# Transposes by DMA, feed-forward in half batches at the lowest priority, and a mask shared by three engines, in a linear-attention and Fourier-mixing kernel

## The chip, the core and the metric

One core of a Trainium2 chip runs the whole program. The time is the device time of one execution in microseconds. For the kernel before it is 328.99 us, the median of three runs from 327.69 to 329.06.

## What is computed

The reference first runs a linear attention over four batches, eight heads, 768 time steps and a head dimension of 48. A state of 48x48 per head decays by w and takes in the outer product of k and v at each step:

```python
for t in range(S):
    cur = einsum('bhd,bhe->bhde', u * k[t], v[t])
    y[t] = einsum('bhd,bhde->bhe', r[t], state + cur)
    state = w * state + einsum('bhd,bhe->bhde', k[t], v[t])
```

The heads are then laid side by side, 384 columns, and go through a Fourier mixer and a feed-forward of width 1536:

```python
mixed = real(fft(fft(x, axis=1), axis=2))
u = x + mixed
un = (u - mean(u)) / sqrt(var(u) + 1e-6)
out = u + maximum(un @ w_ch1, 0) @ w_ch2
```

Inputs and output are float32.

## The kernel before

The kernel is written with a scheduler that takes the program as written, gives each instruction a priority by its place, and sets a fixed order of instructions for each engine ahead of time. Engines then run their own list in order and wait on semaphores. A tile pool with `bufs=n` gives n buffers, and who wants the next one waits until its last reader is done.

Attention goes in chunks of 128 time steps, six to a batch (`attention`, L163). A chunk loads k, r and v for all heads, 192 KB each, on SP's DMA queue (L175 to L177). DVE multiplies k by falling and r by rising powers of the decay (L180 KW, L181 RW), ACT casts v (L183), and POOL makes the diagonal term in three products (L185, L186, L190) with a sum by DVE between them (L188 DE). TensorE transposes KW and RW (L194, L196), and ACT copies the results out of PSUM (L198, L199, L201); for each pair of heads the transposed keys KB hold one head's rows and zeros for the other. TensorE makes the products of keys and queries (L208 A_ps), DVE multiplies both halves by a triangular mask (L211 MA), and TensorE adds up y from the state and the masked products (L217, L220). The next state is made in PSUM and scaled by DVE (L225, L229, L231 Sst). DVE adds the diagonal term (L233 X). From the fourth chunk on DVE also folds the finished chunk with the one three before it by sums and differences (L237 to L241, EO and XF), which halves the work of both Fourier steps.

The mixer (`mixer`, L245) makes the first Fourier step with 18 matmuls against tables (L254), ACT copies the results (L256 TT), and DVE makes a mirrored copy (L259 TR). Then for each of six blocks of 128 rows it runs the second step on TensorE (L273 to L277), and DVE adds the input (L279 UF), takes mean and variance (L282, L284), and norms (L287, L289 UN), with the root on ACT (L286); TensorE transposes the normed rows (L293) and ACT copies them (L294 UNT). The feed-forward of the whole batch follows: 72 matmuls into ReLUs on ACT (L300, L302 HT), 72 more (L306), and for each block a sum by DVE (L309 osb) and a store (L310).

What sets the order: the program emits attention of batch 0, the load of tables and weights, and then for each batch the attention of the next batch and the mixer of this one. The output tiles of the mixer's matmuls share three PSUM buffers (`mm`).

Of the kernel before, what the change touches and what calls it, by code (L numbers as in the profile page):

```python
# [9 lines left out]
AluOp = mybir.AluOpType  # L10
# [5 lines left out]
B = 4  # L16
H = 8
# [45 lines left out]
def kernel(  # L63
# [13 lines left out]
    inp = ctx.enter_context(tc.tile_pool(name="inp", bufs=7))  # L77
    ap_ = ctx.enter_context(tc.tile_pool(name="ap", bufs=3))
    bp = ctx.enter_context(tc.tile_pool(name="bp", bufs=2))
    psA = ctx.enter_context(tc.tile_pool(name="psA", bufs=1, space=bass.MemoryType.PSUM))  # L80
# [9 lines left out]
    wrow = cp.tile([128, H, D], F32, name="wrow")  # L90
    nc.sync.dma_start(out=wrow, in_=w.partition_broadcast(128))
    wT = cp.tile([128, NP], F32, name="wT")
    nc.vector.memset(wT, 1.0)
    wv = w.rearrange("(p a) d -> a d p", a=2)
    nc.scalar.dma_start(out=wT[0:D, :], in_=wv[0])
    nc.scalar.dma_start(out=wT[64:64 + D, :], in_=wv[1])
    urow = cp.tile([128, H, D], F32, name="urow")
    nc.scalar.dma_start(out=urow, in_=u.partition_broadcast(128))
    ident = cp.tile([128, 128], BF16, name="ident")
    nc.scalar.dma_start(out=ident, in_=id_c.ap())  # L100
    mtri = cp.tile([128, 128], BF16, name="mtri")
    nc.scalar.dma_start(out=mtri, in_=mtri_c.ap())
# [10 lines left out]
    lw = cp.tile([128, H, D], F32, name="lw")  # L113
    nc.scalar.activation(lw, wrow, Act.Ln)
    wpp = cp.tile([128, H, D], F32, name="wpp")
    wpn = cp.tile([128, H, D], F32, name="wpn")
    nc.scalar.activation(wpn, lw, Act.Exp, scale=ncol[:, 0:1])
    nc.scalar.activation(wpp, lw, Act.Exp, scale=icol[:, 0:1])  # L118
    lwT = cp.tile([128, NP], F32, name="lwT")
    nc.scalar.activation(lwT, wT, Act.Ln)  # L120
    wdec = cp.tile([128, NP], F32, name="wdec")
    nc.scalar.activation(wdec, lwT, Act.Exp, scale=float(L))
    WD = cp.tile([128, NP, 2, D], F32, name="WD")
    nc.gpsimd.memset(WD, 0.0)
# [3 lines left out]


    NB = 3  # L130
    RWs, KWs, KBs = [], [], []
    for i in range(NB):
        t = cp.tile([128, H, 64], BF16, name=f"RW{i}")
        nc.gpsimd.memset(t[:, :, D:64], 0.0)
        RWs.append(t)
        t = cp.tile([128, H, 64], BF16, name=f"KW{i}")
        nc.gpsimd.memset(t[:, :, D:64], 0.0)
        KWs.append(t)
    for i in range(2):
        t = cp.tile([128, NP, 2, 128], BF16, name=f"KB{i}")  # L140
        nc.gpsimd.memset(t, 0.0)
        KBs.append(t)
# [20 lines left out]
    def attention(b):  # L163
# [4 lines left out]
        for q in range(NQ):  # L168
# [9 lines left out]
            KW = KWs[i % NB]  # L178
            RW = RWs[i % NB]
            nc.vector.tensor_tensor(out=KW[:, :, 0:D], in0=kt, in1=wpn, op=AluOp.mult)  # L180
            nc.vector.tensor_tensor(out=RW[:, :, 0:D], in0=rt, in1=wpp, op=AluOp.mult)  # L181
            V = ap_.tile([128, H, D], BF16, name="V")
            nc.scalar.copy(V, vt)  # L183
            T1 = ap_.tile([128, H, D], F32, name="T1")
            nc.gpsimd.tensor_tensor(out=T1, in0=rt, in1=kt, op=AluOp.mult)  # L185
            nc.gpsimd.tensor_tensor(out=T1, in0=T1, in1=urow, op=AluOp.mult)  # L186
            DE = ap_.tile([128, H], F32, name="DE")
            nc.vector.reduce_sum(out=DE, in_=T1, axis=AX.X)  # L188
            TT = ap_.tile([128, H, D], BF16, name="TT")
            nc.gpsimd.tensor_tensor(out=TT, in0=V, in1=DE.unsqueeze(2).to_broadcast([128, H, D]), op=AluOp.mult)  # L190

            tp = psA.tile([128, 2, NP, 128], BF16, name="tp", bufs=1)
            for p in range(NP):
                nc.tensor.transpose(tp[:, 0, p, :], KW[:, 2 * p:2 * p + 2, :].rearrange("t h d -> t (h d)"), ident)  # L194
            for p in range(NP):
                nc.tensor.transpose(tp[:, 1, p, :], RW[:, 2 * p:2 * p + 2, :].rearrange("t h d -> t (h d)"), ident)  # L196
            KB = KBs[i % 2]
            nc.scalar.copy(KB[0:64, :, 0, :], tp[0:64, 0, :, :])  # L198
            nc.scalar.copy(KB[64:128, :, 1, :], tp[64:128, 0, :, :])  # L199
            RT = ap_.tile([128, NP, 128], BF16, name="RT")  # L200
# [147 lines left out]
```

## Time and profile before

| | |
|---|---|
| median of three runs | 328.99 us |
| profiled execution, its own time | 329.58 us |
| span of the profiled execution | 327.8 us |
| mean granted clock of TensorE | 0.77 |
| busy: TensorE, DVE, ACT, POOL | 220.3, 182.4, 134.9, 81.6 us |
| DMA moved | 23.14 MB, mostly in pieces under 512 B |

How to read it: the span runs from the first instruction to the last. A group of instructions shows its line, engine, operation, output and inputs, count, the busy time in us and the mean of one in ns, and then how long the engine stood idle just before them and what ended that. The chain of waits is followed back from the last instruction, at each step to what released it; its rows show start, length and the piece of work. A matmul's busy time overlaps that of its neighbours, so the time of a run of matmuls is read from the chain. A window's row shows its length, the busy time (and count) of TensorE, its weight loads, DVE, ACT and POOL, the granted clock, the DMA engines' share and GB/s.

### The profile page before, as it was taken

How to read it: one execution, taken by the hardware profiler on the slowest of the kernel's cores; microseconds unless marked ns; L12 is line 12 of the kernel's file. 1: busy time of each engine (PE TensorE's matmuls, PEld its weight loads, DVE VectorE, ACT ScalarE, POOL GpSimd, SP SyncE). 2: the span in 40 equal slices, each digit the busy share in tenths (PEclk: the TensorE clock that was granted, in tenths of full speed). 3: DMA queues.
4: the chain of work that ended last, by engine and by line, in shares of the span. 5: the costliest groups of instructions: out<-in, count | busy, mean ns of one | idle time of the engine just before them, and what ended most of it. 6: DMA issues, size and time to landing. Idle time of an engine off the chain costs nothing.

```text
span 327.8 us, 4361 instructions
## 1 busy us (share of the span) xinstructions
PE 220.3 (67%) x1616; PEld 145.2 (44%) x1616; DVE 182.4 (56%) x374; ACT 134.9 (41%) x272; POOL 81.6 (25%) x92
## 2 busy tenths in 40 slices
PE   0375467653666479996583799944459995446995
PEld 0365244442545256664462566622235652223662
DVE  0989598989989780249894502594430124442022
ACT  4552245633444239237452492331128504113910
POOL 5795365665437442012120200100000000000000
PEclk9999765965555559999757599995558998555999
DMA  7999999992447010120000001200000020000012
GB/s 151 218 187 186 269 206 194 221 184 50 98 86 155 1 24 2 48 98 0 2 1 0 2 0 50 97 0 0 2 0 0 25 97 24 0 0 3 0 48 96
DMA packets 81796, 23.14 MB, mean 71 GB/s; under 512 B 76144, under 2 KB 81008, under 8 KB 81776
## 3 DMA queue, kind: packets, MB, share of 16 engines
q1 hardware_dynamic: 78912, 20.26, 27.6%
q0 software_dynamic: 2016, 2.36, 4.4%
q10 hardware_dynamic: 848, 0.26, 0.3%
q8 instruction: 12, 0.20, 0.2%
q14 instruction: 8, 0.07, 0.1%
HBM read 20.52 MB, written 4.72 MB: 77 GB/s over the span
## 4 chain that ended last, share of the span: by engine, by line
PE 49%; DVE 28%; ACT 7%; DMA 7%; SPq 5%; issue 3%; ACTq 0%; DVEq 0%
PE mm L300 16%; PE mm L306 14%; DMA vt<-in_v_dram 4%; DVE MA L211 4%; PE mm L273 4%; DVE UF L279 3%; DVE UN L289 3%; DVE st L282 3%; PE mm L293 3%; DVE RW L181 3%; PE A_ps L208 2%; ACT RT L201 2%; SPq L175 2%; PE mm L277 2%; DVE KW L180 2%
## 5 line engine op out<-in xcount | busy, mean ns | idle before, releaser
L309 DVE TENSOR_TENSOR osb<-mm,UF 128x384 f32<-128x384 f32 x24 | 13.4, 558 | 87.7 <-PE mm L306 84.9
L300 PE MATMUL mm<-UNT,W 128*128 128x384 bf16 x288 | 54.3, 355 | 0.0
L302 ACT ACTIVATE HT<-mm 128x384 bf16<-128x384 f32 x96 | 46.8, 490 | 6.7 <-PE mm L300 6.5
L190 POOL TENSOR_TENSOR TT<-V,DE 128x384 bf16<-128x384 bf16 x24 | 20.6, 859 | 111.2 <-DVE X L233 48.2
L306 PE MATMUL mm<-W,HT 128*128 128x384 bf16 x288 | 47.5, 326 | 0.0
L293 PE MATMUL mm<-ident,UN 128*128 128x128 bf16 x72 | 12.0, 303 | 44.8 <-DVE UN L289 44.8
L300 PEld LDWEIGHTS <-W 128*128 128x128 bf16 x288 | 30.3, 106 | 21.8 <-issue 6.2
L306 PEld LDWEIGHTS <-HT 128*128 128x128 bf16 x288 | 28.2, 98 | 18.6
L208 PE MATMUL A_ps<-RT,KB 128*128 128x128 bf16 x192 | 21.3, 269 | 21.9 <-ACT RT L201 21.3
L211 DVE TENSOR_TENSOR MA<-A_ps,mtri 128x512 bf16<-128x512 f32 x48 | 31.4, 679 | 5.8 <-PE A_ps L208 5.8
L198 ACT COPY KB<-tp 64x512 bf16<-64x512 bf16 x24 | 13.9, 578 | 44.4 <-PE tp L196 42.4
L185 POOL TENSOR_TENSOR T<-rt,kt 128x384 f32<-128x384 f32 x24 | 27.5, 1144 | 16.8 <-DMA rt<-in_r_dram 12.9
L293 PEld LDWEIGHTS <-UN 128*128 128x128 bf16 x72 | 6.1, 126 | 51.6 <-DVE UN L289 51.1
L208 PEld LDWEIGHTS <-KB 128*128 128x128 bf16 x192 | 17.1, 121 | 25.4 <-issue 16.4
L279 DVE TENSOR_TENSOR UF<-mm,X 128x384 f32<-128x384 f32 x24 | 13.3, 554 | 26.5 <-PE mm L277 26.5
L186 POOL TENSOR_TENSOR T<-T,urow 128x384 f32<-128x384 f32 x24 | 26.9, 1124 | 1.5
L194 PE MATMUL tp<-ident,KW 128*128 128x128 bf16 x96 | 13.9, 294 | 18.6 <-DVE KW L180 16.0
L183 ACT CAST V<-vt 128x384 bf16<-128x384 f32 x24 | 12.2, 515 | 34.5 <-PE y_ps L220 22.6
L286 ACT ACTIVATE rstd<-mv,eps_t 128x1 f32<-128x1 f32 x24 | 7.1, 295 | 42.3 <-DVE mv L284 42.2
L294 ACT COPY UNT<-mm 128x384 bf16<-128x384 bf16 x24 | 11.5, 478 | 28.5 <-PE mm L293 28.5
L181 DVE TENSOR_TENSOR RW<-rt,wpp 128x384 bf16<-128x384 f32 x24 | 22.1, 920 | 0.5 <-ACT wpp L118 0.3
L180 DVE TENSOR_TENSOR KW<-kt,wpn 128x384 bf16<-128x384 f32 x24 | 21.8, 915 | 0.0
(65 smaller groups left out, 355.6 us busy)
## 6 DMA issues: line engine op xcount, KB each, us to landing
kt<-in_k_dram SPq DMA_DIRECT2D x24, 192.0 KB, 3.6
rt<-in_r_dram SPq DMA_DIRECT2D x24, 192.0 KB, 3.8
vt<-in_v_dram SPq DMA_DIRECT2D x24, 192.0 KB, 3.7
out_dram<-osb SPq DMA_DIRECT2D x24, 192.0 KB, 1.8
W<-in_moe_w_ch_dram POOLq DMA_DIRECT2D x6, 384.0 KB, 8.4
hid_t<-hid_c SPq DMA_DIRECT2D x1, 576.0 KB, 9.9
te_t<-te_c SPq DMA_DIRECT2D x1, 289.5 KB, 13.4
to_t<-to_c SPq DMA_DIRECT2D x1, 288.0 KB, 9.0
```

Of the source, the lines that this page charges most:

```text
L180: nc.vector.tensor_tensor(out=KW[:, :, 0:D], in0=kt, in1=wpn, op=AluOp.mult)
L181: nc.vector.tensor_tensor(out=RW[:, :, 0:D], in0=rt, in1=wpp, op=AluOp.mult)
L185: nc.gpsimd.tensor_tensor(out=T1, in0=rt, in1=kt, op=AluOp.mult)
L186: nc.gpsimd.tensor_tensor(out=T1, in0=T1, in1=urow, op=AluOp.mult)
L190: nc.gpsimd.tensor_tensor(out=TT, in0=V, in1=DE.unsqueeze(2).to_broadcast([128, H, D]), op=AluOp.mult)
L208: nc.tensor.matmul(A_ps[:, hh, :], lhsT=KB[:, p, hh % 2, :], rhs=RT[:, p, :], start=(hh == 0), stop=(hh == 3), skip_group_check=True)
L211: nc.vector.tensor_tensor(out=MA, in0=A_ps, in1=mtri.unsqueeze(1).to_broadcast([128, 4, 128]), op=AluOp.mult)
L279: nc.vector.tensor_tensor(out=UF[:, blk, :].rearrange("p (m a) -> p a m", a=2), in0=ps, in1=X[:, blk, :].rearrange("p (m a) -> p a m", a=2 ...
L293: nc.tensor.transpose(tps[:, dt, :], UN[:, dt * 128:(dt + 1) * 128], ident)
L300: nc.tensor.matmul(ps, lhsT=W1[:, dt, ft * 128:(ft + 1) * 128], rhs=UNT[:, dt, sh * 384:(sh + 1) * 384], start=(dt == 0), stop=(dt == 2))
L302: nc.scalar.activation(out=HT[:, ft, sh * 384:(sh + 1) * 384], in_=ps, func=Act.Relu)
L306: nc.tensor.matmul(ps, lhsT=HT[:, ft, sb * 128:(sb + 1) * 128], rhs=W2[:, ft, :], start=(ft == 0), stop=(ft == 11))
```

## The change

Eleven things change.

1. Keys and queries are written into one tile KR of twelve 128-column pieces, four for pairs of keys and eight for single queries with zeros in the other head's rows, and one DMA on SP's queue transposes it into KRT. The eight transposes of a chunk on TensorE and three copies on ACT go.
2. The R product is made in two halves (L176).
3. The products of keys and queries become four matmuls of 256 columns in place of eight of 128; the state's part of y becomes eight of 48 columns in place of four of 96.
4. The second half of the mask goes by an ACT copy (L204 AC) and a select on POOL (L205) instead of DVE.
5. From batch 1 on the fold runs once per batch, in four wide instructions.
6. The mixer's blocks go in halves of three: one root, one reciprocal and one scaled mean for three blocks (L282 to L285), the norm on ACT (L289), and one DMA transpose for the half (L291 UNT).
7. The feed-forward takes half a batch at a time (`mlp`).
8. Attention of later batches and the mixer (`fourier`) are emitted under a raised priority; attention of batch 0, the load of tables, and the feed-forward are not. The feed-forward of a batch is emitted one round later.
9. `mm` has four PSUM buffers instead of three; input tiles have five instead of seven.
10. The masks and u load on SP's queue after the first chunk, the decay's transposed rows on POOL's queue.
11. The decay's logarithm is taken in one ACT instruction of 388 columns.

The core of the diff:

```diff
-    inp = ctx.enter_context(tc.tile_pool(name="inp", bufs=7))
+    inp = ctx.enter_context(tc.tile_pool(name="inp", bufs=5))
...
+            K = KR[:, 0:4, :]
+            nc.vector.tensor_tensor(out=K.rearrange("t p (a d) -> t p a d", a=2)[:, :, :, 0:D],
+                                    in0=kt.rearrange("t (p a) d -> t p a d", a=2),
+                                    in1=wpn.rearrange("t (p a) d -> t p a d", a=2), op=AluOp.mult)
+            for a in range(2):
+                nc.vector.tensor_tensor(out=KR[:, 4 + a:12:2, a * 64:a * 64 + D], in0=rt[:, a::2, :],
+                                        in1=wpp[:, a::2, :], op=AluOp.mult)
...
+            nc.sync.dma_start_transpose(out=KRT, in_=KR.rearrange("t c d -> t (c d)"))
...
+                if g == 0:
+                    nc.vector.tensor_tensor(out=MA, in0=A_ps, in1=mtri.unsqueeze(1).to_broadcast([128, 4, 128]),
+                                            op=AluOp.mult)
+                else:
+                    AC = wp.tile([128, 4, 128], BF16, name="AC", bufs=2)
+                    nc.scalar.copy(AC, A_ps)
+                    nc.gpsimd.affine_select(out=MA, in_=AC, pattern=[[0, 4], [1, 128]], base=0,
+                                            channel_multiplier=-1, compare_op=AluOp.is_gt, fill=0.0)
...
+            for j in range(3):
+                nc.scalar.activation(out=UN[:, j, :], in_=UF[:, j, :], func=Act.Identity, scale=rstd[:, j:j + 1],
+                                     bias=nm[:, j:j + 1])
+            nc.sync.dma_start_transpose(out=UNT.rearrange("p j c t -> p (j c) t"),
+                                        in_=UN.rearrange("p j d -> p (j d)"))
...
-    st = attention(0)
-    load_tables()
-    for b in range(B):
-        nxt = attention(b + 1) if b + 1 < B else None
-        mixer(b, *st)
-        st = nxt
+    xs = [attention(0)]
+    load_tables()
+    hs = []
+    for b in range(B + 1):
+        with tc.high_priority(offset=5000):
+            if b + 1 < B:
+                xs.append(attention(b + 1))
+            if b < B:
+                hs.append(fourier(b, *xs[b]))
+        if b > 0:
+            for sh in range(2):
+                mlp(b - 1, sh, *hs[b - 1][sh])
```

What this moves, at the places of which the prediction speaks. On SP's queue before, the tables te, to and hid load right behind batch 0's chunks, and each chunk's kt, rt and vt follow:

```order
L175 DMA kt_462<-in_k_dram 128x8x48
L176 DMA rt_461<-in_r_dram 128x8x48
L177 DMA vt_463<-in_v_dram 128x8x48
L152 DMA te_t_120<-te_c 128x1158
L153 DMA to_t_121<-to_c 128x1152
L154 DMA hid_t_122<-hid_c 128x2304
L175 DMA kt_536<-in_k_dram 128x8x48
L176 DMA rt_535<-in_r_dram 128x8x48
```

Now SP's queue has, in the middle of batch 1, transposes of one chunk's KR between the loads of chunks six or seven further on:

```order
L181 DMA_TRANSPOSE KRT_588<-KR2_99 128x12x128
L165 DMA vt_1044<-in_v_dram 128x8x48
L163 DMA kt_1101<-in_k_dram 128x8x48
L164 DMA rt_1100<-in_r_dram 128x8x48
L165 DMA vt_1102<-in_v_dram 128x8x48
L181 DMA_TRANSPOSE KRT_646<-KR0_95 128x12x128
L163 DMA kt_1159<-in_k_dram 128x8x48
L164 DMA rt_1158<-in_r_dram 128x8x48
```

and the tables stand behind kt and rt of the very last chunk (kt_1900), with transposes of batches 2 and 3 behind them:

```order
L163 DMA kt_1900<-in_k_dram 128x8x48
L164 DMA rt_1899<-in_r_dram 128x8x48
L140 DMA te_t_104<-te_c 128x1158
L141 DMA to_t_105<-to_c 128x1152
L142 DMA hid_t_106<-hid_c 128x2304
L181 DMA_TRANSPOSE KRT_1169<-KR1_97 128x12x128
L165 DMA vt_1785<-in_v_dram 128x8x48
L181 DMA_TRANSPOSE KRT_1227<-KR2_99 128x12x128
L181 DMA_TRANSPOSE KRT_1629<-KR0_95 128x12x128
```

So the tables moved from ahead of batch 1 to behind all chunks' kt and rt. On DVE before, behind the last chunk's X, the blocks of a mixer go one by one from UF to UN:

```order
L233 TENSOR_TENSOR X_2100<-y_ps_2480,TT_2451 128x384
L259 COPY TR_2529<-TT2_2498 128x768
L237 TENSOR_TENSOR EO_2101<-X_2100 128x384
L238 TENSOR_TENSOR EO_2101<-X_2100 128x384
L279 TENSOR_TENSOR UF_2533<-mm_2535,X_1316 128x2x192
L239 TENSOR_TENSOR XF_2102<-EO_2101 128x2x192
L241 TENSOR_TENSOR XF_2102<-EO_2101 128x2x192
L282 BN_STATS st_2543<-UF_2533 128x6
L284 BN_AGGR mv_2545<-st_2543 128x2
L287 RECIPROCAL rstd_2547<-rstd_2547 128x1
L289 TENSOR_SCALAR UN_2550<-UF_2533,mv_2545,rstd_2547 128x384
```

Now on DVE, around the last chunk's X (y_ps_1931), stands the output sum osb of the feed-forward of batch 0; only osb_1471 of 24 comes ahead of it:

```order
L310 TENSOR_TENSOR osb_1471<-mm_1458,UF_840 128x384
L226 TENSOR_TENSOR X_1615<-y_ps_1873,TT_1859 128x384
L200 TENSOR_TENSOR MA_1922<-A_ps_1919,mtri_94 128x512
L226 TENSOR_TENSOR X_1615<-y_ps_1931,TT_1917 128x384
L310 TENSOR_TENSOR osb_1487<-mm_1474,UF_840 128x384
L236 TENSOR_TENSOR EO_1616<-X_1615 128x1152
L237 TENSOR_TENSOR EO_1616<-X_1615 128x1152
L239 TENSOR_TENSOR XF_1617<-EO_1616 128x6x192
L240 TENSOR_TENSOR XF_1617<-EO_1616 128x6x192
L310 TENSOR_TENSOR osb_1503<-mm_1490,UF_840 128x384
```

Twelve osb stood ahead of the last X before (batches 0 and 1); one does now. Where the tables are first needed, DVE has the fold of batch 1 (EO, XF) and then the TR copy of batch 0, with the product of chunk kt_1619 ahead of them:

```order
L186 TENSOR_REDUCE DE_1232<-T1_1229 128x8
L172 TENSOR_TENSOR KR0_95<-kt_1619,wpn_86 128x8x48
L236 TENSOR_TENSOR EO_468<-X_467 128x1152
L237 TENSOR_TENSOR EO_468<-X_467 128x1152
L239 TENSOR_TENSOR XF_469<-EO_468 128x6x192
L240 TENSOR_TENSOR XF_469<-EO_468 128x6x192
L256 COPY TR_836<-TT2_805 128x768 x3
```

That product frees the buffer for which the load of kt_1900, and so the tables behind it, waits.

234 lines of the change are left out of this document (108 added, 126 removed).

## Prediction

> **What bounds the kernel now.** I read the page first, then the busy time of the engines by stage, then the chain of waits in order of time, and last the groups of instructions. The page gives the sums:
>
> ```profile
> span 327.8 us, 4361 instructions
> PE 220.3 (67%) x1616; PEld 145.2 (44%) x1616; DVE 182.4 (56%) x374; ACT 134.9 (41%) x272; POOL 81.6 (25%) x92
> ```
>
> No engine is busy for the whole span, so the limit changes. The stages (length, then busy us of each engine, granted clock, DMA share, GB/s) say where:
>
> ```profile
> 0.00:36.00 36.00, 14.21 (x140) 12.46 (x140) 23.82 (x40) 14.02 (x25) 24.48 (x37) 1.00 1.06 198
> 36.00:76.00 40.00, 25.37 (x240) 17.72 (x240) 35.39 (x63) 18.44 (x36) 23.28 (x23) 0.68 0.96 194
> 76.00:120.00 44.00, 25.14 (x196) 19.11 (x197) 39.51 (x79) 17.08 (x34) 21.21 (x20) 0.50 0.38 75
> 145.00:185.00 40.00, 24.69 (x247) 18.73 (x244) 33.87 (x79) 19.56 (x41) 7.38 (x8) 0.73 0.02 6
> 270.00:298.00 28.00, 12.68 (x70) 7.28 (x69) 12.79 (x34) 7.19 (x17) 0.00 (x0) 0.60 0.02 7
> ```
>
> While attention runs (36 to 120, 145 to 185) DVE is the limit: 108.8 of 124 us, 88%. The first 76 us also keep the DMA engines full, at about 196 GB/s. From 270 to 298 nothing is even half busy. The chain of waits tells what that is, and what lies between the stages:
>
> ```profile
> 132.87 11.70 PE mm L306 x72
> ...
> 186.66 11.42 PE mm L300 x69
> ...
> 269.98 3.06 ACT TT L256 x6
> ...
> 273.71 0.57 DVE UF L279
> 274.30 0.57 DVE st L282
> ...
> 275.64 0.49 DVE UN L289
> ...
> 276.18 0.50 PE mm L293 x3
> ...
> 277.99 0.57 DVE UF L279
> ...
> 324.02 0.56 DVE osb L309
> ```
>
> Feed-forward: 72 matmuls of L306 take 11.70 us, 0.163 us each, and L300 the same (11.42 for 69). Four batches of 144 are 94 us in which PE alone works. The mixer: one block goes UF, statistics, UN, transpose, and the next UF starts 4.28 us later (273.71 to 277.99); six blocks run one after the other. Behind the last feed-forward matmul come 3.8 us (324.02 to the span's end).
>
> **The change part by part.** The order of the instructions divides the new program into two stages. Stage A ends with the last chunk's y matmul: on PE 57 of the 576 feed-forward matmuls stand ahead of it and 519 behind, and of the mixer batches 0 and 1 ahead, 2 and 3 behind. DVE does nearly everything else in A. So time = A + B, and the feed-forward fills little of A although PE has room there.
>
> *Stage A on DVE*, from these groups (busy us, mean ns):
>
> ```profile
> L211 DVE TENSOR_TENSOR MA<-A_ps,mtri 128x512 bf16<-128x512 f32 x48 | 31.4, 679 | 5.8 <-PE A_ps L208 5.8
> L181 DVE TENSOR_TENSOR RW<-rt,wpp 128x384 bf16<-128x384 f32 x24 | 22.1, 920 | 0.5 <-ACT wpp L118 0.3 <-DMA rt<-in_r_dram 0.2
> L180 DVE TENSOR_TENSOR KW<-kt,wpn 128x384 bf16<-128x384 f32 x24 | 21.8, 915 | 0.0
> L279 DVE TENSOR_TENSOR UF<-mm,X 128x384 f32<-128x384 f32 x24 | 13.3, 554 | 26.5 <-PE mm L277 26.5
> L282 DVE BATCH_NORM_STATS2 st<-UF 128x6 f32<-128x384 f32 x24 | 13.3, 556 | 0.5
> L233 DVE TENSOR_TENSOR X<-y_ps,TT 128x384 bf16<-128x384 f32 x24 | 13.1, 547 | 2.3 <-PE y_ps L220 2.1
> L188 DVE TENSOR_REDUCE DE<-T 128x8 f32<-128x384 f32 x24 | 12.9, 538 | 0.0
> L231 DVE TENSOR_TENSOR Sst<-u_ps,WD 128x384 bf16<-128x384 f32 x20 | 10.9, 544 | 1.8 <-PE y_ps L217 1.0 <-PE u_ps L229 0.7
> L238 DVE TENSOR_TENSOR EO<-X 128x384 bf16<-128x384 bf16 x12 | 5.6, 468 | 0.0
> L239 DVE TENSOR_TENSOR XF<-EO 128x384 bf16<-128x384 bf16 x12 | 5.3, 438 | 0.0
> L259 DVE COPY TR<-TT 128x768 bf16<-128x768 bf16 x12 | 4.9, 418 | 2.3 <-ACT TT L256 2.0
> L241 DVE TENSOR_TENSOR XF<-EO 128x384 bf16<-128x384 bf16 x12 | 4.8, 399 | 0.0
> L237 DVE TENSOR_TENSOR EO<-X 128x384 bf16<-128x384 bf16 x12 | 4.5, 375 | 0.0
> L284 DVE BATCH_NORM_AGGREGATE mv<-st 128x2 f32<-128x6 f32 x24 | 4.3, 177 | 0.5
> ```
>
> K product as before, 21.8. The R product becomes 48 halves: 0.46 each if it scales with its width, 0.92 if it doesn't at all, so 22 to 44. mv, nearly empty, takes 0.18, and with that as a fixed part a half takes 0.55; I take 0.50, hence 24. One mask of two stays: 15.7. DE, X and Sst stay: 36.9. Attention is 98.4. The fold is 20.2 (5.6 + 4.5 + 5.3 + 4.8); three of its four batches lie in A, 15.2, and wide instructions save a little: 14. Two of four batches of UF, st, mv and TR are half of 35.8, 17.9, with 1.4 for eight small ones at mv's 0.177. Sum: 132 us. The K and R rows hold a stall inside them:
>
> ```profile
> 44.25 1.10 DVE KW L180
> ...
> 61.20 0.47 DVE KW L180
> ```
>
> The same instruction takes 1.10 or 0.47, by my reading as POOL is busy or not. POOL does more than before, so I keep the means and count no gain.
>
> *Start.* The first product ran at
>
> ```profile
> 9.28 0.56 DVE L181 TENSOR_TENSOR RW<-rt,wpp 128x384 bf16<-128x384 f32 x1 [0.32 <-ACT wpp L118]
> ```
>
> Now ACT has the cast of V, which waits for vt, ahead of the logarithm of the weights; everything queued on ACT waits with it. I put this at 1.2 us, a guess that enters the sum as it is: 10.5.
>
> *Waits.* At the 88% of the windows above, 132 us of DVE take 150. One stall comes on top: the tables load behind the last chunks' loads, whose buffers wait for DVE, and soon after DVE stops at the TR copy, which needs 18 matmuls and six ACT copies made from those tables. A landing between the 1.8 and 8.4 of the DMA rows further on, 5; 18 matmuls at half clock, twice 0.163, 5.9; the last copy, 0.5; less 4.9 of folding meanwhile: 7 us. A = 10.5 + 150 + 7 = 168.
>
> *Mask by ACT and POOL.* Each chunk adds an ACT cast of 512 columns (0.51 per 384 in the chain: 0.68) and a POOL select, which the trace doesn't show:
>
> ```profile
> L190 POOL TENSOR_TENSOR TT<-V,DE 128x384 bf16<-128x384 bf16 x24 | 20.6, 859 | 111.2 <-DVE X L233 48.2 <-DVE mv L284 27.1 <-DVE rstd L287 19.2
> L185 POOL TENSOR_TENSOR T<-rt,kt 128x384 f32<-128x384 f32 x24 | 27.5, 1144 | 16.8 <-DMA rt<-in_r_dram 12.9 <-DVE DE L188 3.8
> L186 POOL TENSOR_TENSOR T<-T,urow 128x384 f32<-128x384 f32 x24 | 26.9, 1124 | 1.5
> L141 POOL MEMSET KB<- 128x1024 bf16 x2 | 1.8, 948 | 0.0
> ```
>
> Per 512 columns: 0.47 by the memset, 1.53 by L185. I take 1.0, as one operand lies between none and two. POOL then has 75.0 + 24 = 99 us of A's 168: hidden. At 1.5 it has 111 and is hidden too. ACT loses three copies of a chunk and gains the cast; nothing waits for it.
>
> *Transposes by DMA.* Each chunk sends 128x1536 bf16, 384 KB, through SP's queue between the loads. No transpose is in the trace. The nearest rows:
>
> ```profile
> kt<-in_k_dram SPq DMA_DIRECT2D x24, 192.0 KB, 3.6
> out_dram<-osb SPq DMA_DIRECT2D x24, 192.0 KB, 1.8
> W<-in_moe_w_ch_dram POOLq DMA_DIRECT2D x6, 384.0 KB, 8.4
> ```
>
> Loads move 198 GB/s with the engines full, so 192 KB hold them 0.99 us and a chunk's three loads 2.97. At that rate a transpose holds them 1.98 us (lower end). The W row has the same 384 KB and lands after 8.4 (upper end, though its wait in line is in it). I take 2.0, nearest to the loads of the same queue: 24 x (2.97 + 2.0) = 119 us, under the 157 that A leaves after its start. The cover ends where 24 x (2.97 + t) exceeds 157: t = 3.6. Behind a waiting transpose stand the next chunks' loads and, at the end of A, the tables. Removed on PE are eight transposes per chunk and three per block; PE was not the limit there, so nothing counts.
>
> The Trainium skill, "VectorE: DVE Perf Modes", section "The three transpose paths", puts a 128x128 transpose at 1309 ns by DMA against 390 on TensorE and advises TensorE where the output may go to PSUM. Twelve blocks one after the other would be an estimated 15.7 us, and the sum 10.5 + 24 x 18.67 + 113.6 = 572. The skill's "Advanced Engine Details and Errata", "X-Bar Transpose (TRN2)", says the opposite, as fast as a regular DMA, which is my 2.0; no run here shows either yet.
>
> *Stage B.* 519 matmuls x 0.163 = 84.6. Mixers 2 and 3 stand between them: the first step as in the chain (269.45 to 273.71 there; 4.2 us, held by six ACT copies of 0.51), then six blocks without the 4.28 us loop, since the norm and the transpose come later and feed-forward matmuls run meanwhile. A block's 768 columns twice are 0.65 us at L306's rate, 3.9 for six, at most six UFs slower: 5. Together 2 x 9.2 = 18.4. The UN products (6 x 0.49 per batch) now run on ACT among the ReLUs that pace L300: 5. End 3.8. B = 111.8. If that cover failed and the loop came back, it would cost 2 x 6 x 4.28 = 51 less the 10 counted.
>
> *Sum.* 168 + 111.8 = 279.8 against the profiled span of 327.8. The profiled execution took 329.58, 1.8 more than its span, and 0.2% more than the median of 328.99. 279.8 + 1.8 = 281.6: I say 282.
>
> **The rivals.** *The DMA queue paces A.* For: it was full for 76 us with loads alone. Against: before, the loads ran ahead of need; here they spread over A. With t = 5, A = 10.5 + 24 x 7.97 = 202 and the time 202 + 111.8 + 1.8 = 316.
>
> *Slower: the transpose holds the queue beyond 5.6 us.* One mechanism: SP's queue takes transposes and loads in order, and a slow transpose keeps loads, hence DVE, hence all else waiting. It decides where A exceeds 329.6 - 113.6 = 216, so 205.5 / 24 - 2.97 = 5.6 us. At 8.4, A is 283 and the time 397. Against: 8.4 includes queueing behind full engines. "VectorE: DVE Perf Modes" of the Trainium skill, "The three transpose paths", lies on this side.
>
> *Better than counted.* If DVE has no gaps and the tables come early, A = 143; with mixers at column rate B = 102; time 246. Against: DVE never passed 90% here.
>
> *It doesn't do what it says.* The feed-forward has the lowest priority but 519 of its matmuls run after attention, as serially as before; that is already in the sum. If also the mixer chain stayed exposed (41 us), the time would be 323; the order speaks against that.
>
> **How the numbers follow.** Forecast 0.62 (DVE paces A). DMA paces A, t between 3.6 and 5.5: 0.18. Transpose above 5.7: 0.11. Better than 256: 0.06. No change (t near 5.6, or the chain exposed): 0.03. Range: 256 is DVE busy at 95% with no table stall and no ReLU term (10.5 + 139 + 106.8); 316 is t = 5. It holds the first two cases, 0.80. Faster 0.62 + 0.18 + 0.06 = 0.86, within 0.5% 0.03, slower 0.11; half a per cent is about what a measurement of this kernel tells from no change.
>
> **What would show it.** A ends near 168 us with DVE about 88% busy until then; a transpose takes near 2 us of the queue, and DVE's idle time at MA is small; PE is full from there with two breaks of about 9 us; TR in the first mixer waits about 7 us. I am wrong if SP's or the DMA queue's share of the chain in A is large, if the transpose row shows over 3.6 us, or if UN or UNT ends PE's waits in B.

## The result, and the profile after

The changed kernel takes 293.87 us (median of four, 292.54 to 296.78) against 329.02 us for the kernel before in the same comparison: ratio 0.895, 95% interval 0.887 to 0.903. The profiled execution took 292.54 us for a span of 290.8. Forecast were 282 us and a range of 256 to 316. Medians in this document take in every execution, also the slow one of e5 below, which took 334.80 us where the other three took 286.12 to 287.07.

The profiled spans differ by 37 us, and one place shows where they came from: the last X of attention, at which stage A ends, before and then after (times of the first and the last start):

```profile
L233 DVE TENSOR_TENSOR X<-y_ps,TT x24: 536/546/558, 18.0 to 217.6; 128x384 bf16<-128x384 f32 x24
```

```profile
L226 DVE TENSOR_TENSOR X<-y_ps,TT x24: 527/554/559, 23.0 to 181.6; 128x384 bf16<-128x384 f32 x24
```

Stage A ends 36 us earlier. What follows (B) has the same length, 110.2 us before (327.8 - 217.6) and 109.2 after.

This does not mean that attention became faster. Before, 288 feed-forward matmuls started ahead of the last X, now 59 do. At 0.163 us each the 229 that moved are 37 us, which is all by which A is shorter (an estimate, which takes them as run alone). The gain is that B takes them in at the same length: its feed-forward is 84 us instead of 47, so all else in it, with two mixers in both kernels, is 25 us instead of 63. Which part of the change did that (the halves, the norm on ACT, the order) was not taken apart.

The page of after, first its sums, then busy tenths in 40 slices, then the share of the two large DMA queues:

```profile
span 290.8 us, 3776 instructions
PE 178.5 (61%) x1336; PEld 110.2 (38%) x1336; DVE 152.2 (52%) x318; ACT 105.5 (36%) x208; POOL 97.5 (34%) x113
PE   0034123011643264098654697999699996999995
DVE  0494459816977589339799885519210290201202
DMA  6899999999988999910962409310501104201102
q1 hardware_dynamic: 126448, 32.32, 53.8%
q0 software_dynamic: 2080, 2.36, 5.4%
```

PE is nearly full from slice 24 on. In the first 17 slices it is mostly under half busy, DMA is full, and DVE is not. By stage (length, then busy us of PE, PEld, DVE, ACT, POOL, granted clock, DMA share, GB/s), the last row being A from its first product to its end:

```profile
12.00:36.00 24.00, 8.00 (x71) 5.02 (x71) 15.77 (x28) 2.93 (x6) 13.80 (x17) 1.00 1.10 179
36.00:76.00 40.00, 10.17 (x87) 6.93 (x87) 25.59 (x46) 5.28 (x10) 25.03 (x27) 1.00 1.04 198
76.00:120.00 44.00, 16.65 (x157) 11.35 (x158) 33.67 (x61) 8.16 (x15) 25.87 (x28) 1.00 0.97 188
11.25:182.10 170.85, 77.86 (x714) 50.07 (x715) 121.06 (x238) 45.90 (x90) 89.27 (x100) 0.95 0.84 158
```

No engine is busy for more than 71% of A: DVE works 121.06 of 170.85 us and stands idle for 49.8. Before, it was busy for 88% of the stretches in which attention ran. Most of the idle time lies early: 31.3 us of it ahead of the twelfth X, which starts at 110.7 us. In the kernel before, the twelfth X started at 81.5 us, with 8.2 us idle since 11.25. What DVE waited for in A (total, times, longest), and three waits that lie behind it:

```profile
DVE DE L186 <- POOL TT L188: 10.2, 5, 5.2
DVE TR L256 <- ACT TT L253: 9.0, 1, 9.0
DVE X L226 <- PE y_ps L214: 8.2, 9, 1.9
DVE MA L200 <- PE A_ps L195: 6.3, 4, 2.4
DVE KR L172 <- DMA KRT<-KR: 4.6, 3, 3.0
...
PEld L195 <- DMA KRT<-KR: 33.8, 16, 7.0
PE mm L251 <- DMA te_t<-te_c: 9.3, 1, 9.3
ACT V L179 <- DMA vt<-in_v_dram: 26.0, 6, 15.4
```

One wait is that of the tables (TR, 9.0 us, from te_t). The others are smaller, and behind them stand two things: a chunk's transpose, for which PE's weight loads waited 33.8 us, and late loads: the longest wait of DE, 5.2 us, ends with a V whose cast had waited 15.4 us for vt. Two stretches show it best:

```profile
54.00:69.50 15.50, 1.32 (x10) 0.66 (x10) 6.36 (x11) 1.53 (x3) 13.61 (x15) 1.00 1.03 204
118.00:123.50 5.50, 0.01 (x1) 0.00 (x1) 0.60 (x1) 0.00 (x0) 0.00 (x0) 1.00 1.06 250
```

In the second all engines stop until the tables land. In the first, POOL alone is busy most of the time. SP's rows there show why: eight loads of vt are issued from 57.66 us on, and three transposes only behind them. DVE stood from 57.6 to 62.89 for the first of these vt, PE until 69.47 for the first KRT.

```profile
57.66 7.30 SPq L165 DMA_DIRECT2D vt<-in_v_dram  x8
...
65.01 5.88 SPq L181 DMA_TRANSPOSE KRT<-KR  x3
```

The transposes themselves (median us from issue to landing), beside the chain's end (start, us):

```profile
KRT<-KR SPq DMA_TRANSPOSE x24, 4.1
UNT<-UN SPq DMA_TRANSPOSE x8, 3.2
```

```profile
243.31 3.08 PE mm L301 x18
246.40 5.85 PE mm L307 x36
252.25 5.85 PE mm L301 x36
...
281.50 5.86 PE mm L307 x36
287.36 0.02 issue
287.38 0.56 DVE osb L310
```

Stage B runs at the forecast's rate: 36 matmuls in 5.85 us, 0.163 each, without a break between these runs. PE's only wait in it (182 us to the end) is

```profile
PE mm L301 <- ACT HT L303: 4.6, 4, 1.4
```

### The profile page after: what moved, and what is told of

Its sections match the earlier page's. It is cut to its first block, busy times and chain, and to the rows that moved or that the text cites. A ratio compares the mean times of both kernels' runs of the same rounds, so it can differ in the third digit from the quotient of the medians.

```text
span 290.8 us, 3776 instructions
## 1 busy us (share of the span) xinstructions
PE 178.5 (61%) x1336; PEld 110.2 (38%) x1336; DVE 152.2 (52%) x318; ACT 105.5 (36%) x208; POOL 97.5 (34%) x113
## 3 DMA queue, kind: packets, MB, share of 16 engines
q1 hardware_dynamic: 126448, 32.32, 53.8%
## 5 line engine op out<-in xcount | busy, mean ns | idle before, releaser
L310 DVE TENSOR_TENSOR osb<-mm,UF 128x384 f32<-128x384 f32 x24 | 13.3, 555 | 68.6 <-PE mm L307 68.4
L195 PE MATMUL A_ps<-KRT 128*128 128x256 bf16 x96 | 22.7, 381 | 30.9 <-DMA KRT<-KR 28.6
L204 ACT CAST AC<-A_ps 128x512 bf16<-128x512 f32 x24 | 14.0, 585 | 60.4 <-PE A_ps L195 60.4
L176 DVE TENSOR_TENSOR KR<-rt,wpp 128x192 bf16<-128x192 f32 x48 | 26.0, 573 | 3.5 <-DMA rt<-in_r_dram 3.2
L172 DVE TENSOR_TENSOR KR<-kt,wpn 128x384 bf16<-128x384 f32 x24 | 18.7, 784 | 15.6 <-ACT wpn L111 9.8
L205 POOL TENSOR_SCALAR_AFFINE_SELECT MA<-AC 128x512 bf16<-128x512 bf16 x24 | 16.8, 702 | 26.0 <-ACT AC L204 21.1
L195 PEld LDWEIGHTS <-KRT 128*128 128x128 bf16 x96 | 10.4, 125 | 38.3 <-DMA KRT<-KR 33.8
L214 PE MATMUL y_ps<-V,MA 128*128 128x48 bf16 x192 | 12.4, 205 | 15.6 <-DVE MA L200 9.2
L253 ACT CAST TT<-mm 128x386 bf16<-128x386 f32 (+1 forms) x24 | 12.4, 594 | 22.5 <-PE mm L251 22.5
L200 DVE TENSOR_TENSOR MA<-A_ps,mtri 128x512 bf16<-128x512 f32 x24 | 16.4, 682 | 7.6 <-PE A_ps L195 6.3
L186 DVE TENSOR_REDUCE DE<-T 128x8 f32<-128x384 f32 x24 | 13.1, 545 | 12.0 <-POOL TT L188 10.2
```

The lines of the kernel that those rows point to most:

```text
L172: nc.vector.tensor_tensor(out=K.rearrange("t p (a d) -> t p a d", a=2)[:, :, :, 0:D], in0=kt.rearrange("t (p a) d -> t p a d", a=2), in1=w ...
L176: nc.vector.tensor_tensor(out=KR[:, 4 + a:12:2, a * 64:a * 64 + D], in0=rt[:, a::2, :], in1=wpp[:, a::2, :], op=AluOp.mult)
L195: nc.tensor.matmul(A_ps[:, 2 * pp:2 * pp + 2, :], lhsT=KRT[:, p, :], rhs=KRT[:, 4 + 2 * p:6 + 2 * p, :], start=(pp == 0), stop=(pp == 1), ...
L200: nc.vector.tensor_tensor(out=MA, in0=A_ps, in1=mtri.unsqueeze(1).to_broadcast([128, 4, 128]), op=AluOp.mult)
L205: nc.gpsimd.affine_select(out=MA, in_=AC, pattern=[[0, 4], [1, 128]], base=0, channel_multiplier=-1, compare_op=AluOp.is_gt, fill=0.0)
```

## The experiments

Twelve kernels were run, each an edit of the changed kernel. A comparison has its own runs of the kernel before; so kernels are compared by their ratios to it. The table has them all, with the start of the last X, what the span has behind it (B), and DVE's busy and idle time from 11.25 us to that X's end:

| kernel | median us | ratio, 95% interval | last X | B | DVE busy / idle in A |
|---|---|---|---|---|---|
| before | 329.02 | 1 | 217.6 | 110.2 | 147.4 / 59.4 |
| changed | 293.87 | 0.895 (0.887 to 0.903) | 181.6 | 109.2 | 121.1 / 49.8 |
| e1 thin v | 290.13 | 0.881 (0.877 to 0.884) | 180.1 | 107.7 | 122.2 / 47.2 |
| e2 two transposes | 316.77 | 0.962 (0.952 to 0.971) | 203.3 | 108.7 | 122.4 / 70.2 |
| e6 weights late | 303.65 | 0.923 (0.918 to 0.927) | 191.6 | 110.5 | 121.0 / 59.9 |
| e8 transposes by ACT | 313.52 | 0.952 (0.948 to 0.956) | 200.9 | 109.9 | 121.7 / 68.4 |
| e9 look-ahead 2 | 293.33 | 0.893 (0.888 to 0.898) | 185.2 | 104.9 | 127.9 / 46.7 |
| e10 look-ahead 3 | 297.96 | 0.905 (0.899 to 0.912) | 186.1 | 111.4 | 132.1 / 43.3 |
| e3 tables in the middle | 282.52 | 0.860 (0.856 to 0.864) | 176.3 | 106.6 | 121.8 / 43.9 |
| e5 transposes by TensorE | 286.69 | 0.872 (0.868 to 0.877) | 169.7 | 114.7 | 125.5 / 33.6 |
| e4 mask on DVE | 304.92 | 0.928 (0.921 to 0.934) | 196.1 | 105.5 | 134.3 / 51.2 |
| e11 half of R | 291.90 | 0.887 (0.881 to 0.894) | 181.6 | 109.5 | 108.3 / 62.5 |
| e7 no priority | 274.12 | 0.833 | 189.4 | 81.7 | 136.3 / 42.5 |
| e12 tables and TensorE | 281.30 | 0.855 (0.850 to 0.860) | 164.6 | 114.9 | 126.9 / 27.1 |

e1's first product ran only at 14.33 us, so 3.1 us of its idle time are its later start. For e7 no interval was given; its four executions, 269.86 to 276.94 us, all lie below every execution of the others (280.23 the lowest).

**First question: do bytes, DVE or SP's order pace A?** e1 takes bytes away and leaves the issues:

```
-            nc.sync.dma_start(out=vt, in_=v[b, :, sl, :].rearrange("h p d -> p h d"))
+            nc.sync.dma_start(out=vt[:, 0, :], in_=v[b, 0, sl, :])
-            nc.scalar.copy(V, vt)
+            nc.scalar.copy(V, vt[:, 0:1, :].to_broadcast([128, H, D]))
```

> Of v only the first head is loaded (24 KB instead of 192 KB a chunk) and ACT spreads it over the eight heads of V, so the output leaves out seven of the eight heads of v; every DMA is still issued, and SP's order is nearly the same. Removed are 24 x 168 KB, at 196 GB/s 20.6 us of the 16 DMA engines. Three theories of what paces stage A of the changed kernel (293.9 us; A ended at 182 us in its profile). The bytes (loads, transposes and weights keep the engines full until about 123 us): A ends about 20 us earlier, 274 us (270 to 279). DVE, as predicted, with the transfers hidden: 291 to 294 us. The order on SP's queue (instructions that wait there for KR or for a buffer, with the next issues behind them): the order and the waits stay, so no more than 5 us, 289 to 294.

Measured 290.13 us: 1.6% less than the changed kernel by the ratios, not 7%. The edit also moved two casts of V ahead of the logarithm on ACT, which is why its first product ran 3.1 us later; from its first product on, A gained 4.6 us. That is still far from 20: the bytes alone do not pace A. e1's row for 36 to 76 us is

```profile
36.00:76.00 40.00, 10.33 (x93) 6.95 (x94) 28.23 (x47) 5.19 (x10) 23.68 (x26) 1.00 0.93 176
```

with 176 GB/s where the changed kernel had 198, and DVE at 28.23 us instead of 25.59.

e2 adds bytes and issues:

```
+            KR2 = wp.tile([128, 11, 128], BF16, name="KR2", bufs=1)
+            nc.sync.dma_start_transpose(out=KR2, in_=KR[:, 0:11, :].rearrange("t c d -> t (c d)"))
```

> Every KR is transposed a second time by DMA (11 of its 12 pieces, 352 KB) into a tile that nobody reads; the result stays as it is. At 2.2 us of all engines for 384 KB (66 us more of the queue for 32 transposes than before the change) that is 24 x 0.917 x 2.2 = 48 us of transfers, and 24 x 1.8 = 43 us in which SP issues. The bytes pace A: 340 us (328 to 346). DVE paces A: by the prediction's cover (24 x (2.97 + t) against 157, so t = 3.6) the doubled t of 4.0 goes 10 us over it, so 300 to 308. SP's order paces A: 320 to 340. It separates DVE from the other two, not these from each other.

Measured 316.77 us, 23 more (20 by the faster two of its four executions), between the cases: more than the 14 at most for DVE alone, less than the 34 to 52 for the bytes. A became 21.7 us longer, DVE's busy time stayed (122.4) and its idle time rose by 20.4. So a further transpose is not hidden, although neither bound holds in full. Two side effects blur the price: te now stood earlier on SP's queue (issued at 88.90 us), and KR2 has one buffer, for which SP waited 8.7 us in six waits.

e6 moves the weights:

```
+    def load_weights(X):
+        for dt in range(3):
+            nc.gpsimd.tensor_copy(W1[0:1, dt, 0:1], X[0:1, 5, 0:1])
+            nc.gpsimd.tensor_copy(W2[0:1, 4 * dt, 0:1], X[0:1, 5, 0:1])
```

> W1 and W2 (15.7 us of the engines on POOL's queue) are loaded only after the last X of batch 1, instead of during batch 0: six copies of one element on POOL make the loads wait. The result stays as it is. SP's queue is untouched. The bytes pace A: 15.7 us of transfers leave the time in which the engines are full, 279 us (276 to 284), unless feed-forward matmuls then wait for weights in A, which costs nothing as few stand there. DVE paces A: 291 to 294. SP's order paces A: 291 to 294.

Measured 303.65 us, 10 slower, which no theory gave. The weights now came at 107 to 113 us, right ahead of the tables, and the wait for these grew from 9.3 to 21.9 us, seen in e6's row:

```profile
PE mm L256 <- DMA te_t<-te_c: 21.9, 1, 21.9
```

So the whole time of this run doesn't price the bytes: they still stood ahead of the tables, in a worse place. Up to there it does say something. Without the weights among the first loads the fifth X started at 39.8 us instead of 47.2, and the twelfth at 104.4 instead of 110.7: 6 to 7 us, which came with 15.7 us of transfers moved. By e1 and e6 together, bytes pace a part of A, and not most of it.

e8 puts the transposes on another queue:

```
-            nc.sync.dma_start_transpose(out=KRT, in_=KR.rearrange("t c d -> t (c d)"))
+            nc.scalar.dma_start_transpose(out=KRT, in_=KR.rearrange("t c d -> t (c d)"))
```

> The 24 transposes of KR are issued by ACT instead of SP (1.8 us each in the changed kernel, so up to 43 us of ACT, which is busy for 54 of A's 182 us); loads are no longer queued behind a transpose that waits for KR, nor transposes behind loads that wait for a buffer. The result and the bytes stay as they are. The bytes pace A: 290 to 296. DVE paces A: 290 to 296. SP's order paces A: the waits on SP for KR, A_ps and y_ps in A (about 60 us in all, part of them overlapping other idle time) go, 273 to 284.

Measured 313.52 us, 20 slower. It does not tell whether SP's order costs anything, for it put new waits in the place of the old. SP's rows in A of e8:

```profile
SPq L291 <- DMA KRT<-KR: 38.4, 3, 18.9
SPq L165 <- ACT V L179: 29.5, 7, 17.9
SPq L163 <- DMA KRT<-KR: 15.6, 3, 8.4
```

SP waited for transposes of the other queue to land before it issued its own (L291), and a transpose landed after 5.7 us (median) instead of 4.1. Inconclusive for its question.

**Second question: SP's bunches, the tables, or the transpose itself?** e9 and e10 keep the loads of chunk i behind the transpose of chunk i - 2 or i - 3:

```
+            with tc.issue_after(trs[i - 2]) if i >= 2 else nullcontext():
                 nc.sync.dma_start(out=kt, in_=k[b, :, sl, :].rearrange("h p d -> p h d"))
...
-            nc.sync.dma_start_transpose(out=KRT, in_=KR.rearrange("t c d -> t (c d)"))
+            ti = nc.sync.dma_start_transpose(out=KRT, in_=KR.rearrange("t c d -> t (c d)"))
```

> The loads of chunk i are issued only behind the transpose of chunk i - 2 on SP (a constraint on the order of issue; no wait for the transpose to land). The bytes and the result stay as they are; the order of SP becomes at most two chunks of loads between transposes instead of up to eight, and the tables are issued right behind chunk 1's loads. Three runs have weakened the theory that the bytes pace A (21 us of transfers less gave 4 us, not 20), and doubled transposes cost 23 us where DVE alone would have cost 10. Theory now: the order on SP; in the changed kernel eight loads each of k, r and v stand ahead of three transposes, and between 53 and 69 us DVE stands still because those transposes are issued only from 65.0 on. By that theory A ends 12 to 20 us earlier, 270 to 282 us, the tables' 9 us in it. If the bytes pace A: the tables move 6 us of transfers to the front and only the gap of 9 us goes: 284 to 294. If DVE paces A: 284 to 288, the table stall alone. If a shorter look-ahead starves DVE of loads: over 296.

> As the run before, with the transpose of chunk i - 3: at most three chunks of loads between transposes, and the tables late, behind chunk 17's loads, as in the changed kernel. The result stays as it is. SP's order paces A: between the changed kernel and the look-ahead of two, 278 to 288 us. The bytes or DVE pace A: 290 to 296, since neither bytes nor tables move.

Measured 293.33 and 297.96 us: neither differs from the changed kernel by more than the intervals allow, and e9 had its tables at 8.30 us. The theory of the bunches, which expected 270 to 288, fell in these two. DVE's busy time in A also grew, by 6.8 and 11.0 us; most of that is the R products, 34.4 and 36.0 us in sum instead of 27.5. With few loads ahead SP waits for the products instead, with the next loads behind it, and DVE for A_ps; of e9:

```profile
SPq L183 <- DVE KR L178: 60.3, 22, 6.8
```

```profile
DVE MA L203 <- PE A_ps L198: 24.0, 13, 4.3
```

e3 moves the tables alone, by a dependence on the third X of batch 0:

```
+    def load_seq(X):
+        for t in (te_t, to_t, hid_t):
+            nc.gpsimd.tensor_copy(t[0:1, 0, 0:1], X[0:1, 2, 0:1])
```

> The three loads of the tables (1.15 MB, 6 us at 196 GB/s) are issued after the third X of batch 0, among the loads of chunk 6 instead of behind chunk 23's; three copies of one element on POOL set the moment. The result stays as it is. It measures the prediction's table stall (7 us) by itself: PE waited 9.3 us for te in the changed kernel and DVE 9.0 at TR. If the stall is what it costs: 284 to 288 us. If the bytes pace A the 6 us only move, and loads come 6 us later: 288 to 294. SP's order: the bunch of 24 loads ahead of three transposes stays, so no more than the stall: 284 to 288.

Measured 282.52 us, 11 less than the changed kernel; the profiled spans differ by 7.9. That is the stall and a little more. te is issued at 37.70 us instead of 118.98, DVE's idle time in A falls by 5.9, A by 5.3 and B by 2.6, of which 1.1 are 7 more feed-forward matmuls ahead.

e5 gives KR's transposes back to TensorE:

```
+            for g in range(2):
+                tp = ps.tile([128, 6, 128], BF16, name="tp", bufs=1)
+                for c in range(6):
+                    nc.tensor.transpose(tp[:, c, :], KR[:, 6 * g + c, :], ident)
+                nc.scalar.copy(KRT[:, 6 * g:6 * g + 6, :], tp)
```

> KR is transposed by TensorE, six pieces into one tile of PSUM, copied by ACT to KRT, twice a chunk; the transposes of UN stay with the DMA, and mm has three buffers instead of four. The result stays as it is. PE gets 288 transposes more (about 0.1 to 0.16 us each, 29 to 46 us), ACT 48 copies of 768 columns (about 0.9 us, 43 us), both engines less than half busy in A. 53 us of transfers go, and SP issues loads alone. The bytes pace A: 262 to 275. SP's order paces A: 268 to 282, since no transpose waits behind loads. DVE paces A: 288 to 296. If the copies on ACT come into the chain of each chunk: over 296.

Measured 286.69 us: 7 less than the changed kernel, but 5 above what SP's order would give and 1 below DVE's case. Added were (busy us, mean ns)

```profile
L184 PE MATMUL tp<-ident,KR 128*128 128x128 bf16 x288 | 36.4, 277 | 27.8 <-DVE KR L172 13.8 <-ACT KRT L185 7.9 <-DVE KR L176 5.7
L185 ACT COPY KRT<-tp 128x768 bf16<-128x768 bf16 x48 | 38.4, 800 | 39.0 <-PE tp L184 38.4 <-PE y_ps L215 0.4
```

and still A became 11.9 us shorter: DVE was idle for 33.6 us instead of 49.8, and busy for 4.4 us more. ACT's casts of V waited 5.0 us for vt instead of 26.0, so the loads came earlier too. B became 5.5 longer: only 22 feed-forward matmuls stand ahead of the last y, 35 fewer, and 35 x 0.163 = 5.7.

**Third question: is it DVE after all?** e4 gives DVE 24 products more, e11 24 fewer:

```
-                if g == 0:
...
-                    nc.gpsimd.affine_select(out=MA, in_=AC, pattern=[[0, 4], [1, 128]], base=0,
-                                            channel_multiplier=-1, compare_op=AluOp.is_gt, fill=0.0)
+                nc.vector.tensor_tensor(out=MA, in0=A_ps, in1=mtri.unsqueeze(1).to_broadcast([128, 4, 128]),
+                                        op=AluOp.mult)
```

> The whole mask goes back to DVE: 24 products more of 512 columns at 0.68 us, 16.4 us of DVE, and 24 casts on ACT and 24 selects on POOL fewer. The result, the bytes and the order on SP stay as they are. If DVE paces A, as predicted: 16 to 23 us more (16.4 us at a DVE that is busy 72 to 100% of A), 310 to 317 us. If A is paced by no engine's work but by waits between the engines in their fixed orders: 290 to 300, as DVE has some 50 us of waiting in A to put the products into, and the step over ACT and POOL goes.

```
-            for a in range(2):
+            for a in range(1):
                 nc.vector.tensor_tensor(out=KR[:, 4 + a:12:2, a * 64:a * 64 + D], in0=rt[:, a::2, :],
```

> The second of the two R products of a chunk is left out, so the odd heads of R are zero in the result: 24 DVE instructions of 0.57 us, 13.8 us, fewer; the rest, the bytes and nearly all of SP's order stay. If DVE paces A: 14 to 19 us less, 275 to 280 us. If waits between the engines pace A: 288 to 295.

The rows of A, e4 first:

```profile
11.25:196.70 185.45, 83.38 (x728) 52.51 (x729) 134.30 (x263) 33.26 (x66) 72.36 (x77) 0.82 0.79 145
```

```profile
11.25:182.10 170.85, 79.75 (x713) 50.32 (x714) 108.30 (x213) 46.78 (x91) 89.35 (x101) 0.96 0.85 157
```

e11 is the plainest reading of the study: DVE works 12.8 us less, its idle time grows by 12.7, and the last X starts at 181.6 us as before the edit (291.90 us, 2 less, within the intervals). The orders are not quite the same: in e11 three transposes come first on SP, and the first X starts at 29.3 us instead of 23.0; but by the fourth X both are level (43.7 and 43.9), with 20 chunks to come. In the changed kernel DVE's work does not set A. The other direction isn't the mirror of it: 13.2 us more of DVE made A 14.5 us longer, and the kernel 11 us slower (304.92), between the two expectations. So work added lengthened A, and work taken off was refilled by other waits (the table stall at TR was 11.8 us in e11); why the two directions differ was not tested.

**Last: two ways on.** e7 takes the priority of attention and mixers away and keeps all else:

```
-        with tc.high_priority(offset=5000):
+        if True:
             if b + 1 < B:
```

> The high priority of attention and mixers is taken away, everything else of the change stays, and so does the result: 167 instead of 57 of the 576 feed-forward matmuls then stand ahead of the last y on PE, the tables come behind chunk 3's loads, and SP's loads and transposes alternate. By the prediction's sum B loses 110 x 0.163 = 18 us and the table stall 9 us goes while A stays: 262 to 272 us. If feed-forward matmuls hold up attention on PE (they come in runs of 36, 5.9 us): A longer by as much or more than B loses, 282 to 300.

Measured 274.12 us, 2 above the first case and the best of all: 17% less than the kernel before and 20 us less than the change as it was made. Stage A and B of e7:

```profile
11.25:190.00 178.75, 104.10 (x878) 63.46 (x879) 136.27 (x265) 60.23 (x119) 89.68 (x100) 0.89 0.86 158
```

```profile
190.00:271.10 81.10, 74.99 (x459) 44.67 (x457) 20.78 (x50) 39.70 (x84) 0.00 (x0) 0.98 0.20 59
```

A takes in 110 feed-forward matmuls and a whole mixer more (18 UF of 24 come ahead of the last X instead of 12) and becomes only 7.8 us longer; PE works 104 us in it instead of 78. B loses 27.5 us: 110 x 0.163 = 17.9 and the forecast's 9.2 for a mixer are 27.1. e7 also has its tables at 47.72 us, and TR waits 2.4 us in all. How much of the 20 us is the tables, which e3 priced at 11, and how much the filling of A, was not separated. Something else came with the filling: PE's matmuls took less time. The four matmuls of one A_ps took 1.01 to 1.06 us throughout the changed kernel's A up to 110 us, and 0.60 to 0.65 in five of nine between 60 and 127 us of e7.

e12 is e3 and e5 in one.

> The two runs that were faster than the changed kernel in one: tables among chunk 6's loads (282.5 us against 293.9) and KR transposed by TensorE with copies by ACT (286.7). The result stays as it is. If the two gains are apart: 293.9 - 11 - 7, 274 to 279 us. If both remove the same wait: 280 to 286.

Measured 281.30 us, the second case: the two do not add up, and the time can't be told from e3's. A is the shortest of all (last X at 164.6) and DVE 82% busy in it, but B is 114.9 us, 8.3 more than e3's, as 554 feed-forward matmuls are left for it.

## Why the prediction came out as it did

**The number held, and its main reason did not.** 282 was 4% below the measured time. B was forecast at 111.8 us and is 109.2; A at 168 and is 181.6. That A missed by no more than 14 us is luck in part: a sum that was too large covered half of the waiting that was missing. The start was nearly right: the first product ran at 11.25 us (10.5).

**Stage B: right, each term within 2 us.** 519 x 0.163 is the chain's rate (5.85 us for 36). The mixers stand as two breaks of about 7.6 us (193.65 to 201.28, 228.60 to 236.22; 9.2 forecast); PE's only wait in B is that for ACT, 4.6 us, where the UN products on ACT among the ReLUs were put at 5. e7, which moves one mixer and 110 matmuls, changes B by 27.5 us where these terms give 27.1.

**DVE's sum: right as a sum of durations, and used wrongly.** These are the products and the select:

```profile
L176 DVE TENSOR_TENSOR KR<-rt,wpp 128x192 bf16<-128x192 f32 x48 | 26.0, 573 | 3.5 <-DMA rt<-in_r_dram 3.2 <-DMA KRT<-KR 0.3
L172 DVE TENSOR_TENSOR KR<-kt,wpn 128x384 bf16<-128x384 f32 x24 | 18.7, 784 | 15.6 <-ACT wpn L111 9.8 <-DMA KRT<-KR 4.6 <-DMA kt<-in_k_dram 0.9
L200 DVE TENSOR_TENSOR MA<-A_ps,mtri 128x512 bf16<-128x512 f32 x24 | 16.4, 682 | 7.6 <-PE A_ps L195 6.3 <-POOL MA L205 1.1 <-issue 0.2
L205 POOL TENSOR_SCALAR_AFFINE_SELECT MA<-AC 128x512 bf16<-128x512 bf16 x24 | 16.8, 702 | 26.0 <-ACT AC L204 21.1 <-DVE MA L200 2.6 <-PE y_ps L214 2.2
```

K came to 18.8 (forecast 21.8), R to 27.5 (24), the mask to 16.4 (15.7); the select took 0.70 us (1.0) and stayed hidden, as POOL has 89 us of A's 171. R's 27.5 us seem to hold a wait. The view of the tile shows it (shortest, median, longest in ns):

```profile
L176 DVE TENSOR_TENSOR KR<-rt,wpp x48: 343/351/1664, 13.5 to 175.0; 128x192 bf16<-128x192 f32 x48
```

Of these 48, 20 ran while POOL stood still and took 343 to 358 ns; the 26 with POOL busy for over half of their time took 764 on average. That fits the forecast's reading of 1.10 and 0.47; no run took POOL's work away. By that, part of DVE's busy time is waiting too.

The larger error is of another kind. Durations of 135 us in A (132 forecast) are only 121 us of a busy engine, because DVE's recorded instructions overlap:

```profile
84.69 0.86 DVE L172 TENSOR_TENSOR KR<-kt,wpn 128x384 bf16<-128x384 f32 x1
85.48 0.68 DVE L200 TENSOR_TENSOR MA<-A_ps,mtri 128x512 bf16<-128x512 f32 x1
```

The second starts at 85.48, the first ends at 85.55. The step "At the 88% of the windows above, 132 us of DVE take 150" divided a sum of durations by a share of busy time. In one unit it would have been 121 / 0.88 = 138, and A 155.5. The surplus of 12 us hid half of the 26 that were missing.

**What failed: "hidden".** The forecast allowed DVE 18 us of waiting and 7 for the tables; it had 49.8. Two experiments name most of the difference. With KR transposed by TensorE the idle time falls by 16.2 us (e5), and by 16.8 with the tables early in both (e3 to e12); A falls by 12 in each, as DVE's products took longer. So the transposes by DMA, which were counted at nothing, "119 us, under the 157", cost DVE about 16 us of waiting, measured against TensorE's path. Not all of that is a chunk waiting for its own transpose: ACT's waits for vt and DVE's for rt and kt (3.2 and 0.9 us in the changed kernel, none in e5) went with it. The tables cost 9.0 at TR where 7 was said, and 11 in the whole time (e3). With both removed DVE is idle for 27.1 us, near the 25 of the forecast, and busy for 82% of A: that picture is e12's, not the change's. Whether DVE paces A there was not tested.

**By the forecast's own signs.** DVE was busy for 71% of A and not 88. The waits at MA were small as said (7.6 us), TR waited 9.0 us for 7, and neither UN nor UNT ends a wait of PE in B. The transposes' row shows 4.1 us, over the 3.6 that was to mean being wrong; that limit had been worked out for the time a transpose holds the DMA engines, which is 2.2 here; what a chunk waits for is the landing. The chain followed back from the last instruction breaks off at 240 us and says nothing of A.

**The first rival had the place, not the price.** A transpose does hold about 2 us of the engines: q1 went from 27.6% of 327.8 us to 53.8% of 290.8, 66 us more for the 30 pieces of 384 KB that 24 KRT and 8 UNT make, 2.2 each.

```profile
q1 hardware_dynamic: 78912, 20.26, 27.6%
```

At 2.2 that rival's sum leaves A untouched, and the slower rival, which needed over 5.6, did not come near. What it and the forecast both left out is that a chunk waits for its own transpose, 4.1 us from issue to landing, behind whatever SP has ahead of it, with three buffers of KR, and that loads wait behind transposes. e1 and e6 show that fewer bytes help little, e9 and e10 that another order of the loads alone does not, e2 that another transpose costs 0.9 us of A a chunk. Which link of the chunk's chain would have to be shortened to bring DVE's work back as the limit stays open beyond that.

The Trainium skill, "VectorE: DVE Perf Modes", section "The three transpose paths", gives 1309 ns for one 128x128 block. The estimate that twelve blocks follow one another, 15.7 us, is not borne out: a transpose of twelve landed after 4.1 us in the trace. What the Trainium skill says in "Advanced Engine Details and Errata", "X-Bar Transpose (TRN2)", as fast as a regular DMA, is within 11% of the 2.2 us (a load of the same bytes holds the engines 1.98). The advice of the Trainium skill, "VectorE: DVE Perf Modes", section "Rules for kernel authors", to use TensorE where PSUM will do agrees with e5, for DVE's waiting and not for bandwidth.

**Better than counted.** The forecast gave 0.06 to less than 256 us, by tables that come early and a DVE without gaps. Its reason against, that DVE never passed 90%, holds for the windows shown; in the page's 40 slices DVE has ten at 90% or more. Its bound of 256 also leaves out the 1.8 us that the other sums add. No run came there; early tables were worth 11 us, and the 20 of e7, the tables' share in them, came with the step in which the forecast saw no lever, "the feed-forward fills little of A although PE has room there". It took that as given by the order. It was the priority, part of the change, that emptied PE in A.

## What to carry to other kernels

Before a sum of instruction durations is divided by a busy share, add up the durations of a whole profile and see how far they exceed the busy time. A transfer in the middle of each item's chain is not hidden because its queue has room: count its latency and its place in the queue, and name what else the chain can do meanwhile. A priority that keeps filler work behind the critical chain also leaves the idle engine of that stage idle; try the order without it before shortening anything (e7, in which the tables came earlier as well).

## What the runs showed of the hardware

DVE's recorded instructions overlap: counts times means of all its groups add up to 170 us, and the page has it busy for 152.2, so 0.06 us for each of the 318. A DMA share of 1.0 did not mean that bytes alone were the limit: with 20.6 us of transfers fewer (e1) the share from 36 to 76 us was still 0.93.

The granted clock of a row is not to be trusted ahead of the first record of the clock in its trace. From 76 to 100 us it is 1.00 in the changed kernel and 0.50 in e10, at about the same PE time (first the changed kernel, then e10):

```profile
76.00:100.00 24.00, 9.08 (x103) 6.58 (x103) 18.80 (x35) 4.32 (x8) 18.35 (x21) 1.00 0.87 170
```

```profile
76.00:100.00 24.00, 9.51 (x83) 6.27 (x82) 16.86 (x28) 4.39 (x8) 13.62 (x17) 0.50 0.95 184
```

But the four matmuls of one A_ps take the same time in both there, and much less later on. These are the changed kernel's, e10's, and the changed kernel's again:

```profile
86.54 1.03 PE L195 MATMUL A_ps<-KRT 128*128 128x256 bf16 x4
```

```profile
85.93 1.03 PE L198 MATMUL A_ps<-KRT 128*128 128x256 bf16 x4 [4.35 <-DMA KRT<-KR]
```

```profile
141.13 0.60 PE L195 MATMUL A_ps<-KRT 128*128 128x256 bf16 x4
```

They start 213 ns apart in the first two and 109 in the third. The changed kernel's trace holds no record of the clock ahead of 126 us (e10's none ahead of 64); its rows print 1.00 there while its matmuls run at the slower rate. The 1.00 in its rows above is therefore no sign that PE ran at full speed in A.
